# Clearing one column of x^T before it is filled, and forming a combined weight in a stream of its own

## The chip, the cores and the metric

The kernel runs on one core of one Trainium2 chip. The metric is the device time of one execution in microseconds; lower is better. A core has a matrix engine (TensorE, PE in the profile), a vector engine (DVE), a scalar engine (ACT), a general engine (POOL) and a queue processor (SP) that issues DMAs. Each engine works through its own list of instructions in the order in which the program gives them, and an instruction that waits for a semaphore holds up all that stand behind it on its engine.

## What is computed

```python
# q, k, v: (8, 12, 448, 64); w_ch1: (768, 3072); w_ch2: (3072, 768)
scores = q @ k.T / sqrt(64)
x      = (maximum(scores, 0)**2 / 448) @ v          # attention without softmax
x      = x.transpose(0, 2, 1, 3).reshape(8, 448, 768)
u      = x + real(fft(fft(x, axis=1), axis=2))      # Fourier mixing over rows and channels
un     = (u - mean(u)) / sqrt(var(u) + 1e-6)        # over the 768 channels
out    = u + maximum(un @ w_ch1, 0) @ w_ch2
```

## The kernel before

The eight batches go one after the other through attention, mixing, normalization and the feed-forward product (FFN), and the stages of different batches overlap. The FFN works on groups of rows that do not coincide with batches: 384 rows in group 0, 512 in group 1, 384 in group 2 and 256 in each later one.

**Order of the work.** Each activity is a Python generator, here called a stream, that says with `need(engine, duration, deps, bufs)` which engine it wants next, for how long, after which times and with which buffers. A planner (`Streams.run`) picks the piece with the earliest possible start, and among equal starts the one with the lowest rank, and emits its instructions. The planner's clock is its own model; on the chip the engines follow the emitted order, and the semaphores decide when each instruction really starts. So a small edit can change the order of much that comes behind it.

**Attention.** For each batch `b` and each pair of heads `m` (0 to 5), three or fewer score tiles at a time are formed (L734), ACT takes them out of PSUM with a relu (L759, tile `sq`), and DVE or ACT squares them (L774, L771). Eight products with `v` (L716) then give 128 channels of x transposed, in PSUM (`psF`, or `psS` while the FFN's two chains hold both `psF` banks). `leave` in `fold` takes them out, scaled, into `xT` (DVE L553 or ACT L550), in two instructions for the two halves of the sequence. From batch 2 on (`PAR` is 2) each half is written as even and odd positions, 112 of each; the folding that follows reads 113 (`EV`), and column 112 (`EV - 1`) must be zero, since batches 0 and 1 left data there. A DMA transposition then brings each `m` back to row order (SP L650, tile `xn`).

**Folding and mixing.** `halves(b, k)` folds three channel blocks at once: k is 0 for m = 0 to 2 and 1 for m = 3 to 5. It adds and subtracts the halves (DVE L614, L616), then L624 twice, and for k = 1 also L632 and L634, on which the channel transform waits (PE L1210). At batch 2 alone it first clears column 112 of its three blocks (L612). `mix_rows` does the row transform (PE L1024), ACT copies one part (L1036), DVE and POOL form u (L1057, L1059), DVE the statistics (L1066 to L1072), and ACT or POOL the normalized rows (L1085, L1082, tile `un`). These are written to DRAM (`ntop` by SP L1117, `nbot` by POOL L1120) and read back transposed as `unT` (SP L1158); an FFN group starts when its `unT` is there.

**FFN.** The first product (L1445) fills one `psF` bank at a time (there are two), and ACT or DVE takes it out with a relu (L1419, L1417, tile `hT`). Group 0's second product is plain (L1470); groups 1 and 2 form part of theirs by `whole` (L1496), and all other parts are formed by `Pair`, which forms two blocks of rows with seven products of 12 matmuls instead of eight (L1576). Its two chains A and B each keep one `psF` bank; DVE adds what a product gave to the output (L1431), and a chain's next product waits for that add. `Pair` reads sums and differences of blocks of the second weight: `weight_sums` forms them on DVE (L1302, tile `wsum`; the fourth, T[4], lies in the upper half of `hT`). The fourth is formed in twelve blocks after group 1's blocks c = 2 and 3 are done (`upper_free`), and eight of the blocks, which group 2 overwrites, are formed again after its c = 2 (`third_done`). `weight_sums` has rank 6, `halves` 3, the copies ahead of the q and k transpositions (L469, SP L481) 2.

Of the kernel before, what the change touches and what calls it, by code (L numbers as in the profile page):

```python
# [12 lines left out]
ALU = mybir.AluOpType  # L13
# [123 lines left out]
def need(eng, dur, deps=(), bufs=(), ok=None):  # L137
    return eng, dur, list(deps), list(bufs), ok
# [10 lines left out]
def dve(n):  # L149
    return n / 960 + 0.15  # L150
# [6 lines left out]
def dve2(n):  # L157
    return Port(n / 1920 + 0.14)
# [6 lines left out]
def kernel(  # L165
# [9 lines left out]
    nc = tc.nc  # L175
# [7 lines left out]
    JC = FF // 128  # L183
# [9 lines left out]
    PAR, EV = 2, 113  # L193
# [28 lines left out]
    sch = Streams()  # L222
# [68 lines left out]
    half_seq, seq_left, tail_left, half_ready = [None], Cell(), Cell(), Cell()  # L291
# [151 lines left out]
    BX = [Bufs(1) for _ in range(MC)]  # L443
# [79 lines left out]
    def fold(b, m, F, av, give, av_end):  # L523
        one = b < WHOLE
        x, at = xTc[m], av[:, 0:S].rearrange("q (j p) -> q p j", j=4)
        gone = Cell()

        def leave():

            if b < PAR:  # L530
                xa = x[:, 0:HS].rearrange("q (p j) -> q p j", j=4), at[:, 0:R // 2]
                xb = x[:, XH + 1:XH + NS].rearrange("q (p j) -> q p j", j=4), at[:, R - 1:R // 2 - 1:-1, ::-1]
            else:
                split = at.rearrange("q p (h o) -> q o p h", o=2)
                xa = (x[:, 0:256].rearrange("q (o e) -> q o e", o=2)[:, :, 0:R].rearrange("q o (p h) -> q o p h", h=2),
                      split[:, :, 0:R // 2])
                xb = (x[:, XH + 1:XH + 255].rearrange("q (o e) -> q o e", o=2)[:, :, 0:R]
                      .rearrange("q o (p h) -> q o p h", h=2), split[:, :, R - 1:R // 2 - 1:-1, ::-1])
            if b == 0:
                t = yield need("DVE", 2 * dve(HS) + 2 * dve2(NS), [av_end], [BX[m]] + ([BA[m]] if m < 3 else []))  # L540
                for out_, in_ in (xa, xb):
                    nc.vector.tensor_scalar(out_, in_, 1.0 / (64.0 * S), None, op0=ALU.mult)
            else:
                yield need("PE", 0.0, [av_end - LATENCY["PE"]])
                en = "ACT" if sooner(av_end, "ACT", 2 * act(HS), "DVE", 2 * dve(HS)) else "DVE"
                bufs = [BX[m]] + ([BA[m]] if m < 3 and b < PAR else [])
                for out_, in_ in (xa, xb):
                    if en == "ACT":
                        t = yield need(en, act(HS), [av_end], bufs)
                        nc.scalar.activation(out_, in_, AF.Copy, scale=1.0 / (64.0 * S))  # L550
                    else:
                        t = yield need(en, dve(HS), [av_end], bufs)
                        nc.vector.tensor_scalar(out_, in_, 1.0 / (64.0 * S), None, op0=ALU.mult)  # L553
                    bufs = []
                t += LATENCY[en] - LATENCY["DVE"]
            give(t - (0.0 if b else 2 * dve2(NS)))
            if b > 0:
                sch.add(turn_x(b, m, t + LATENCY["DVE"]), (1, 1))
            else:
                x_ready[b][m].t = t + LATENCY["DVE"]  # L560
            gone.t = t
            return t

        if b >= PAR:
            x_gone[b].append(gone)
            sch.add(leave(), (0, 0))
            if m % 3 == 2:
                sch.add(halves(b, m // 3), (3, 3))
            return
        if b == 0:  # L570
            e1 = yield from leave()
        else:
            sch.add(leave(), (0, 0))
            yield need("SP", 0.0, [gone])
            e1 = gone.t + LATENCY["DVE"]
        if one and b:
            e1 = yield need("DVE", 2 * dve2(NS), [e1])
        if m % 3 == 0 and (b == 0 or m == 0):
            trio[:] = [work.tile([128, 3, 2, NS], BF16, name="fold", tag="foldB" if m else "foldA", bufs=1)] + trio[:1]
        f = seq_home[:, SEQ:SEQ + 2 * NS].rearrange("q (t n) -> q t n", t=2) if b and m >= 3 else trio[0][:, m % 3]  # L580
        if not one:
            e1 = yield need("DVE", dve2(NS), [e1])
        nc.vector.tensor_tensor(f[:, 0, :], x[:, 0:NS], x[:, XH:XH + NS], op=ALU.add)
        e1 = yield from next_step(b, "DVE", dve2(NS), e1)
        nc.vector.tensor_tensor(f[:, 1, :], x[:, 0:NS], x[:, XH:XH + NS], op=ALU.subtract)
        F.append(f)
        if b == 0:
            first_folds.append(f)
            f_ready[m].t = e1 + LATENCY["DVE"]
        elif m >= 3:  # L590
            i = m - 3
            e1 = yield need("DVE", (2 if one else 1) * dve2(2 * NS))
            if i == 0:
                trio[:] = [work.tile([128, 3, 2, NS], BF16, name="diff", tag="foldB", bufs=1)]
            t = trio[0][:, i]
            nc.vector.tensor_tensor(t, F[i], f, op=ALU.subtract)
            Bs[b].append(t)
            e1 = yield from next_step(b, "DVE", dve2(2 * NS), e1)
            nc.vector.tensor_tensor(F[i], F[i], f, op=ALU.add)
            As[b].append(F[i])  # L600
            ab_ready[b][i].t = e1 + LATENCY["DVE"]

    x_gone, trio, firsts = [[] for _ in range(B)], [], [None] * B
    BFA, BFB, BFS = Bufs(1), Bufs(1), Bufs(1)

    def halves(b, k):

        x = xT3[k]
        xa, xb = (x[:, :, at:at + 256].rearrange("q m (o e) -> q m o e", o=2)[:, :, :, 0:EV] for at in (0, XH))
        e1 = yield need("DVE", dve2(6 * EV) + 0.1 * (b == PAR), x_gone[b][3 * k:3 * k + 3] + [seq_left], [BFS])  # L610
        if b == PAR:
            nc.vector.memset(x[:, :, EV - 1:EV], 0.0)  # L612
        f = work.tile([128, 3, 2, 2, EV + 1], BF16, name="folds", tag="seqm", bufs=1)
        nc.vector.tensor_tensor(f[:, :, 0, :, 0:EV], xa, xb, op=ALU.add)  # L614
        e1 = yield need("DVE", dve2(6 * EV))
        nc.vector.tensor_tensor(f[:, :, 1, :, 0:EV], xa, xb, op=ALU.subtract)  # L616
        f = f.rearrange("q m t o e -> q (m t) (o e)")
        low = f.rearrange("q c (o e) -> q c o e", o=2)[:, :, :, 0:EH]
        high = f[:, :, 0:2 * EV].rearrange("q c (o e) -> q c o e", o=2)[:, :, :, EV - 1:EH - 2:-1]
        for w, op in enumerate((ALU.add, ALU.subtract)):  # L620
            e1 = yield need("DVE", dve2(12 * EH), [], [(BFA, BFB)[k]] if w == 0 else [])
            if w == 0:
                Y = work.tile([128, 2, 6, 2, EH], BF16, name="fold", tag=("foldA", "foldB")[k], bufs=1)
            nc.vector.tensor_tensor(Y[:, w], low, high, op=op)  # L624
        if k == 0:
            BFS.free.append(e1)
            firsts[b] = Y
            return
        first, second = (y.rearrange("q w c o e -> q (w c o e)") for y in (firsts[b], Y))
        e1 = yield need("DVE", dve2(24 * EH))  # L630
        t = work.tile([128, 24 * EH], BF16, name="diff", tag="seqm", bufs=1)
        nc.vector.tensor_tensor(t, first, second, op=ALU.subtract)  # L632
        e1 = yield need("DVE", dve2(24 * EH))
        nc.vector.tensor_tensor(first, first, second, op=ALU.add)  # L634
        BFB.free.append(e1)
        for y, home in ((first, As), (t, Bs)):
            y = y.rearrange("q (w m t e) -> q w m t e", w=2, m=3, t=2)
            home[b][:] = [y[:, :, m] for m in range(3)]
        for c in ab_ready[b]:
            c.t = e1 + LATENCY["DVE"]  # L640
# [618 lines left out]
    DH = D // 2  # L1259
# [10 lines left out]
    T = [None] * 5  # L1270
    sums = [Cell() for _ in range(5)]
    ffn_begun = [Cell() for _ in range(NGR)]
    unt_left, w2_free, upper_free, third_done = Cell(), Cell(), Cell(), Cell()
# [5 lines left out]
    def weight_sums():  # L1279
# [28 lines left out]
        b11, b12, b21, b22 = (0, 0), (0, 1), (1, 0), (1, 1)  # L1308
# [4 lines left out]
        t2 = yield from home("uA", 4, u_left)  # L1313
# [2 lines left out]
            t2 += yield from home(f"{x}n0", 2, [qk_left])  # L1316
        yield from several(2, t2, t3, b11, ALU.add, [])
        yield from several(1, b12, b12, b11, ALU.subtract, [w2_free])
        yield need("DVE", 0.0, [upper_free])
        t4 = upper(JC * 256, KP, DH)  # L1320
        t4 = [(t4, i) for i in range(KP)]
        yield from several(4, t4, b21, t2, ALU.subtract, [])
        yield need("DVE", 0.0, [third_done])
        T[4], sums[4].t = None, None
        yield from several(4, t4, b21, t2, ALU.subtract, [], JC * 128 // DH)

    def uses():

# [381 lines left out]
```

## Time and profile before

| | us |
|---|---|
| median of 3 runs | 586.08 (585.96 to 586.13) |
| profiled execution, its own time | 588.24 |
| span of the profiled execution | 586.3 |
| PE busy | 571.7 (98%) |
| DVE busy | 412.8 (70%) |
| ACT busy | 330.2 (56%) |
| POOL busy | 137.6 (23%) |

The span runs from the first to the last instruction. The profiled execution is one of its own, 2.16 us over the median. A row of the timeline reads: start, duration, engine, line, operation, output tile and input tile, count, and in brackets the idle time of the engine just before and what ended it. PSUM tiles are `psF` and `psS`.

### The profile page before, as it was taken

Reading aid. Unit: us, or ns where it says so; the run is one execution under the profiler, and the core shown is the slowest. Engines: PE = TensorE matmul, PEld = TensorE weight load, DVE = VectorE, ACT = ScalarE, POOL = GpSimd, SP = SyncE. Lnnn points to the kernel's source line nnn. Section 1 sums busy time; section 2 is a strip of 40 time slices with the busy share of each in tenths; the row PEclk is TensorE's granted clock in tenths of the full one; section 3 lists DMA queues with packets and bytes.
Section 4 is the critical chain, followed back from the end, with each engine's and each line's share of the span. In section 5 each row is a group of like instructions: output and inputs, shape, how many; then the busy total and the mean of one; then the engine's idle time right before and its main releaser. Section 6 shows DMA issues by size and latency. Waiting matters only on the chain.

```text
span 586.3 us, 11457 instructions
## 1 busy us (share of the span) xinstructions
PE 571.7 (98%) x4476; PEld 364.4 (62%) x4476; DVE 412.8 (70%) x929; ACT 330.2 (56%) x503; POOL 137.6 (23%) x190
## 2 busy tenths in 40 slices
PE   8999999999999999999999999999999999999997
PEld 6566556544355446546756667558567686868684
DVE  5978677986679968897899878977946862222222
ACT  5967773687634478777668738766644240404040
POOL 8533121410134211431126132303300230000000
PEclk9999999999999999999999999999999999999999
DMA  9999999875938997599949977995434343131211
GB/s 127 207 210 227 215 226 128 198 108 75 200 48 197 159 179 138 132 193 175 154 103 211 207 139 146 203 164 128 124 75 100 114 144 94 40 91 42 73 36 55
DMA packets 133493, 81.85 MB, mean 140 GB/s; under 512 B 77504, under 2 KB 128704, under 8 KB 133440
## 3 DMA queue, kind: packets, MB, share of 16 engines
q0 software_dynamic: 40320, 33.63, 37.4%
q1 hardware_dynamic: 93120, 47.50, 37.2%
q8 instruction: 35, 0.57, 0.4%
q14 instruction: 18, 0.15, 0.1%
HBM read 62.91 MB, written 26.25 MB: 152 GB/s over the span
## 4 chain that ended last, share of the span: by engine, by line
PE 82%; DVE 8%; ACT 4%; DMA 3%; SPq 1%; issue 1%; POOL 0%; DVEq 0%; POOLq 0%
PE psF L1445 34%; PE psF L1576 24%; PE psS L734 6%; PE psF L716 4%; PE psF L1496 4%; PE psF L1470 3%; PE psS L1210 2%; DVE sq L774 2%; ACT sq L759 2%; DMA xn<-xT 2%; PE psS L716 1%; DMA qkT<-qkr 1%; PE psS L821 1%; PE psS L1024 1%; SPq L1158 1%
## 5 line engine op out<-in xcount | busy, mean ns | idle before, releaser
L1445 PE MATMUL psF<-unT,w 128*128 128x256 bf16 (+2 forms) x1728 | 229.3, 291 | 4.8 <-DVE hT L1417 1.3
L1445 PEld LDWEIGHTS <-w 128*128 128x128 bf16 x1728 | 165.6, 98 | 65.8 <-issue 13.5
L759 ACT ACTIVATE sq<-psS 112x896 bf16<-112x896 f32 x192 | 164.0, 917 | 44.2 <-PE psS L734 44.0
L1419 ACT ACTIVATE hT<-psF 128x512 bf16<-128x512 f32 (+3 forms) x166 | 86.0, 530 | 122.8 <-PE psF L1445 121.4
L774 DVE TENSOR_TENSOR sq<-sq 112x896 bf16<-112x896 bf16 x162 | 102.4, 646 | 16.3 <-ACT sq L759 15.2
L1576 PEld LDWEIGHTS <-hT 128*128 128x128 bf16 x792 | 76.1, 98 | 54.2 <-issue 5.8
L1576 PE MATMUL psF<-w,hT 128*128 128x384 bf16 x462 | 81.5, 326 | 0.3 <-DVE hT L1417 0.2
L1431 DVE TENSOR_TENSOR o<-psF,o 128x384 f32<-128x384 f32 x92 | 50.8, 553 | 42.6 <-PE psF L1576 38.5
L734 PE MATMUL psS<-qkT 64*128 64x448 bf16 (+1 forms) x384 | 51.4, 358 | 1.6 <-ACT sq L759 0.6
L553 DVE TENSOR_SCALAR xT<-psF 128x224 bf16<-128x224 f32 x56 | 19.2, 385 | 28.3 <-PE psF L716 28.2
L1057 POOL TENSOR_TENSOR u<-tp,xn 112x385 f32<-112x385 f32 (+2 forms) x14 | 13.1, 933 | 110.3 <-DVE tp L1039 89.0
L716 PE MATMUL psF<-sq,vn 112*64 112x448 bf16 x312 | 37.0, 358 | 0.0
L376 POOL DMA_DIRECT2D qn<-in_q_dram x21 | 15.7, 748 | 83.1 <-DVE qkr L469 66.1
L1576 PE MATMUL psF<-wsum,hT 128*128 128x384 bf16 x198 | 35.0, 326 | 0.0
L734 PEld LDWEIGHTS <-qkT 64*128 64x128 bf16 (+1 forms) x384 | 15.7, 102 | 28.7 <-issue 21.7
L376 POOL DMA_DIRECT2D vn<-in_v_dram x24 | 17.2, 718 | 65.3 <-PE psS L734 58.6
L716 PEld LDWEIGHTS <-vn 112*64 112x64 bf16 x384 | 17.7, 109 | 21.2 <-issue 13.5
L771 ACT ACTIVATE sq<-sq 112x896 bf16<-112x896 bf16 x30 | 28.6, 957 | 0.5
L1066 DVE BATCH_NORM_STATS2 stats<-u 112x6 f32<-112x384 f32 (+2 forms) x56 | 28.7, 542 | 0.1
L1470 PE MATMUL psF<-w,hT 128*128 128x384 bf16 x144 | 25.1, 326 | 0.0
L1417 DVE TENSOR_SCALAR hT<-psF 128x512 bf16<-128x512 f32 (+3 forms) x38 | 20.4, 550 | 6.3 <-PE psF L1445 5.8
L1085 ACT ACTIVATE un<-u,nmr,rstd 113x768 bf16<-113x768 f32 (+2 forms) x20 | 20.1, 1022 | 8.3 <-DVE nmr L1072 8.2
(166 smaller groups left out, 626.0 us busy)
## 6 DMA issues: line engine op xcount, KB each, us to landing
out_dram<-o SPq DMA_DIRECT2D x56, 192.0 KB
vn<-in_v_dram POOLq DMA_DIRECT2D x24, 224.0 KB, 6.4
qn<-in_q_dram POOLq DMA_DIRECT2D x21, 224.0 KB, 4.6
kn<-in_k_dram POOLq DMA_DIRECT2D x21, 224.0 KB, 6.9
w<-in_moe_w_ch_dram POOLq DMA_DIRECT2D x12, 384.0 KB, 13.2
w<-in_moe_w_ch_dram POOLq DMA_DIRECT2D x4, 1152.0 KB, 27.0
utop<-u SPq DMA_DIRECT2D x12, 336.0 KB
o<-utop SPq DMA_DIRECT2D x16, 192.0 KB
```

The costliest lines, as they stand in the source:

```text
L376: nc.gpsimd.dma_start(out=t, in_=src[b, hs].rearrange("h (p j) d -> p h (j d)", j=4))
L716: nc.tensor.matmul(av[h * Dh:(h + 1) * Dh, 0:S], lhsT=vn[:, c, h0 + h, :], rhs=sq[:, h, :], start=(c == 0), stop=(c == 3))
L734: nc.tensor.matmul(sc[:wide, h, 0:S].rearrange("k (c q) -> k c q", c=4), lhsT=flat[ps, k0:k0 + wide], rhs=qT[ps, m % 2], start=True, stop= ...
L759: nc.scalar.activation(r, sc[:R, :, 0:S], AF.Relu)
L771: nc.scalar.activation(r, r, AF.Square)
L774: nc.vector.tensor_tensor(r, r, r, op=ALU.mult)
L1066: nc.vector.bn_stats(stats[:n, hf, :], u[:n, hf * (D // 2):(hf + 1) * (D // 2)])
L1419: nc.scalar.activation(hs, ps, AF.Relu)
L1431: nc.vector.tensor_tensor(o, pc[:, 0:DH], o, op=ALU.add)
L1445: nc.tensor.matmul(ph[:, i * N:(i + 1) * N], lhsT=w1_sb[m][hf][:, (jj + i) * 128:(jj + i + 1) * 128], rhs=unT[:, m, 0:N], start=(m == 0), ...
L1470: nc.tensor.matmul(pc[:, 0:DH], lhsT=block(j, c), rhs=w2(j, hf), start=(j == 0), stop=(j == JC - 1))
L1576: nc.tensor.matmul(pc[:, 0:DH], lhsT=lhs[i], rhs=rhs[i], start=(start and i == 0), stop=(i == KP - 1), skip_group_check=True)
```

## The change

Three edits:

- At batch 2, `leave` clears column 112 of its own block with a DVE instruction of its own before the two instructions that fill the block, for each m. `halves` no longer clears anything. The buffer `BX[m]`, which the DMA transposition of the batch before gives back, is taken by the clearing instead of by the first filling instruction.
- The fourth combined weight is formed by a stream of its own, `fourth`, of rank 2 instead of 6. `weight_sums` ends once it has added it.
- The two waits in it, for `upper_free` and `third_done`, are put on SP's clock in the planner instead of DVE's. They emit no instruction.

```diff
@@ leave, in fold
                 bufs = [BX[m]] + ([BA[m]] if m < 3 and b < PAR else [])
+                if b == PAR:
+                    yield need("DVE", 0.06, [av_end], [BX[m]])
+                    nc.vector.memset(x[:, EV - 1:EV], 0.0)
+                    bufs = []
                 for out_, in_ in (xa, xb):
@@ halves
-        e1 = yield need("DVE", dve2(6 * EV) + 0.1 * (b == PAR), x_gone[b][3 * k:3 * k + 3] + [seq_left], [BFS])
-        if b == PAR:
-            nc.vector.memset(x[:, :, EV - 1:EV], 0.0)
+        e1 = yield need("DVE", dve2(6 * EV), x_gone[b][3 * k:3 * k + 3] + [seq_left], [BFS])
@@ weight_sums
-        yield need("DVE", 0.0, [upper_free])
+        yield need("SP", 0.0, [upper_free])
         t4 = upper(JC * 256, KP, DH)
         t4 = [(t4, i) for i in range(KP)]
-        yield from several(4, t4, b21, t2, ALU.subtract, [])
-        yield need("DVE", 0.0, [third_done])
-        T[4], sums[4].t = None, None
-        yield from several(4, t4, b21, t2, ALU.subtract, [], JC * 128 // DH)
+
+        def fourth():
+
+            yield from several(4, t4, b21, t2, ALU.subtract, [])
+            yield need("SP", 0.0, [third_done])
+            T[4], sums[4].t = None, None
+            yield from several(4, t4, b21, t2, ALU.subtract, [], JC * 128 // DH)
+
+        sch.add(fourth(), (2, 2))
```

In the order of the built programs, PE's instructions are the same up to the one that starts at 154.18 us in the profile of before, and again from about 322 us to the end. Between the two the same matmuls stand in another order.

## The prediction, made before the changed kernel was run

> **What bounds the kernel now.** I read the page first: the engines' busy time says whether anything but PE can matter.
>
> ```profile
> span 586.3 us, 11457 instructions
> PE 571.7 (98%) x4476; PEld 364.4 (62%) x4476; DVE 412.8 (70%) x929; ACT 330.2 (56%) x503; POOL 137.6 (23%) x190
> ```
>
> PE is idle for 14.6 us in all. The changed program has the same matmuls and the same order of them outside one stretch, so I asked next for the stretch's share (a row gives the stretch, its length, then busy time and count of PE, PEld, DVE, ACT and POOL, the clock and the DMA).
>
> ```profile
> 154.00:322.00 168.00, 164.30 (x1174) 94.91 (x1173) 139.34 (x315) 108.56 (x175) 50.52 (x55) 1.00 0.87 155
> ```
>
> Here PE is idle for 3.70 us at full granted clock. That is the most that the change can bring, 0.6%; what it can cost has no such bound. DVE is busy for 139 of 168 us: a wait on DVE is soon felt.
>
> Then the timeline of the stretch, for PE's gaps. Five make 3.62 us of the 3.70:
>
> ```profile
> 158.54 0.06 DVE L612 MEMSET xT<- 128x3 bf16 x1 [2.68 <-DMA xn<-xT]
> 161.00 0.68 DVE L1417 TENSOR_SCALAR hT<-psF 128x512 bf16<-128x512 f32 x1
> 161.73 4.04 PE L1445 MATMUL psF<-unT,w 128*128 128x512 bf16 x18 [1.26 <-DVE hT L1417]
> 166.13 0.46 PE L1210 MATMUL psS<-chan,fold 128*114 128x193 bf16 x3 [0.36 <-DVE fold L634]
> 204.36 1.14 PE L1445 MATMUL psF<-unT,w 128*128 128x384 bf16 x6 [0.74 <-DVE o L1431]
> 259.23 1.14 PE L1576 MATMUL psF<-w,s 128*128 128x384 bf16 x6 [0.65 <-DVE o L1431]
> 315.19 2.79 PE L1445 MATMUL psF<-unT,w 128*128 128x256 bf16 x24 [0.61 <-DVE mv L1067]
> ```
>
> The first row is what the change touches: the second clearing (m = 3 to 5) writes into blocks that a transposition still reads, so DVE stands still for 2.68 us. The relu at 161.00 waits behind it and holds a `psF` bank, so PE loses 1.26 us, and the folds end late, 0.36 us more. The chain of waits in this stretch says the same:
>
> ```profile
> 152.83 5.55 DMA xn<-xT
> 158.54 0.07 DVE xT L612
> 165.29 0.79 DVE fold L634
> 166.13 2.21 PE psS L1210 x24
> ```
>
> **Part 1: the clearing.** Two instructions of 0.06 us become six, 0.24 us more on DVE, hidden by its idle time. Each stands right before a value block's two exits, and the block that it clears was last read a whole batch earlier, so I expect no wait. The second fold then follows m = 5's exit at once. In the changed order the two relus that DVE takes in group 1's last nine chunks are other ones (the 17th and 21st of 24 instead of the 16th, 17th and 20th), and PE has a value block or scores between. Gain: 1.26 + 0.36 = 1.62 us.
>
> **Part 2: where that time goes.** A PE that doesn't wait only arrives sooner at the next thing. That is group 2's first product, 204.36, which needs `unT`. I walk both sides.
>
> *PE.* Before group 2 the new order holds one value block and two sets of three score tiles more than the old one:
>
> ```profile
> 184.60 0.88 PE psF L716 x8
> 195.53 0.67 PE psS L734 x6
> 192.98 0.48 PE psS L734 x4
> 193.47 2.06 PE psF L1576 x12
> 569.09 13.66 PE psF L1576 x84
> ```
>
> That is 0.88 + 2 x 0.67 = 2.22 us. Taking out the three gaps before (1.26, 0.36, 0.74), PE arrives at 204.36 - 2.36 + 2.22 = 204.2.
>
> *unT.* Its last part comes by this chain:
>
> ```profile
> 187.88 0.16 DVE L1072 SCALAR_TENSOR_TENSOR nmr<-mv,rstd 112x1 f32<-112x1 f32 x1
> 184.97 0.99 POOL L1082 TENSOR_SCALAR un<-u,rstd,nmr 112x768 bf16<-112x768 f32 x1
> 188.13 1.96 POOL L1082 TENSOR_SCALAR un<-u,rstd,nmr 112x768 bf16<-112x768 f32 x1 [2.17 <-DVE nmr L1072]
> 190.37 1.05 POOL L1120 DMA_INDIRECT nbot<-un,backe  x1 [0.28 <-POOL un L1082]
> 195.34 2.51 SPq L1158 DMA_TRANSPOSE unT<-nbot  x1
> 193.29 0.77 POOL L376 DMA_DIRECT2D vn<-in_v_dram  x1 [1.87 <-PE psS L734]
> 195.80 0.94 POOL L376 DMA_DIRECT2D qn<-in_q_dram  x1 [1.74 <-DVE qkr L469]
> ```
>
> L1158 is issued at 195.34 and PE reads at 204.36, 9.02 us later. The gap there is put down to DVE's add, but the transposition may have ended as late as that.
>
> In the new order the second `mix_rows` of batch 2 stands after 60 instead of 42 of the 96 L1496, and the last scale factor behind group 1's last add, two squares and the first pair's sums. Backward from 204.2: 84 products (13.66), two value blocks (1.76), scores (0.48 + 0.67 + 0.48 + 0.67) and four returns to the products (2.06 - 12 x 13.66 / 84 = 0.11 each), 18.2 us, so L1496 ends at 186.0. Then DVE has:
>
> ```profile
> 190.49 0.55 DVE L1431 TENSOR_TENSOR o<-psF,o 128x384 f32<-128x384 f32 x1
> 187.95 0.62 DVE L774 TENSOR_TENSOR sq<-sq 112x896 bf16<-112x896 bf16 x1
> 186.28 0.43 DVE L1560 TENSOR_TENSOR hT<-hT 128x512 bf16<-128x512 bf16 x1
> 187.28 0.29 DVE L1560 TENSOR_TENSOR hT<-hT 128x256 bf16<-128x256 bf16 x1
> 187.69 0.15 DVE L1071 RECIPROCAL rstd<-std 112x1 f32<-112x1 f32 x1
> ```
>
> Two adds, two squares, three sums at 0.43, three at 0.29 and two pairs of 0.15 + 0.16: 5.1 us, so the factor is there at about 191.1 (against 188.04). POOL needs 0.99 to 1.96 us, now issues a q load (0.94) ahead of `nbot`, and pauses 0.28: `nbot` at 193.3 to 194.3. It took 4.97 us from there to L1158 before, so L1158 goes out at 198.3 to 199.3. What a transposition takes when nothing else is in question, the chain shows:
>
> ```profile
> 368.95 5.32 DMA xn<-xT
> 383.78 6.46 DMA qkT<-qkr
> ```
>
> With 5.32 at least and 9.02 at most, `unT` is there between 203.6 and 208.3. PE, ready at 204.2, waits 0 to 4.1 us. I take 1.4: issue at 198.8 and 6.8 us for the transposition, between 6.46 and the old 9.02 and nearer to the first, since the load of v that lay beside it (193.29, after a value block) comes a value block earlier in the new order.
>
> [...]
>
> *The copies.* In the new order the k copy ahead of the q and k transpositions stands before the exit of group 2's first value block, and its L481 behind both L1158 on SP. At another place the trace prices such a wait:
>
> ```profile
> 390.33 0.43 DVE L469 COPY qkr<-kn 112x1024 bf16<-112x1024 bf16 x1 [1.76 <-DMA qkT<-qkr]
> 392.20 1.49 PE L1445 MATMUL psF<-unT,w 128*128 128x256 bf16 x12 [1.02 <-DVE xT L553]
> ```
>
> There PE paid 1.02 us. Here the wait is largely the same time as the wait for `unT`: 0 to 1.02, I take 0.3.
>
> **Part 3: the fourth weight.** Its 20 blocks are the same work on DVE (eleven instructions), earlier in the queue. No product waits for it in the old profile, so nothing is gained by its being early. It now goes ahead of folds, not behind them: the adds that were late before 204.36 and 259.23 stood behind folds and squares, and in the new order the folds stand after them. So 0.74 and 0.65 should go (the first is in PE's arrival above). The moved wait is only in the planner; it can let the first block be queued before the matmuls that it overwrites are done, for 0.5 us at most, while DVE has nothing else.
>
> **Part 4: the rest of the stretch.** The gap of 0.61 comes from a chance:
>
> ```profile
> 311.15 1.80 DVE L1059 TENSOR_TENSOR u<-tp,xn 112x383 f32<-112x383 f32 x1
> 295.76 0.55 DVE L1059 TENSOR_TENSOR u<-tp,xn 113x383 f32<-113x383 f32 x1
> ```
>
> The same instruction takes 1.80 or 0.55 us, by what POOL does beside it. Such things will lie elsewhere: of the 1.26 us after 204.36 (0.65 + 0.61) I expect 0.7 to be lost again, 0 to 2.
>
> **Sum.** -1.62 - 0.74 + 1.4 + 0.3 - 1.26 + 0.7 = -1.22 us. The profiled execution took 588.24 us (the span and 1.94 around it) and becomes 587.02; the median of the runs lies 2.16 lower, 586.08, and becomes 584.86: 584.9. With every term at its lower bound it would be 582.5, with every term at its upper 589.6. A measurement of this kernel tells 0.2% (1.17 us) from no change, so the forecast stands right at that edge.
>
> **The rivals.**
>
> *`unT` in time.* L1158 lands before 204.2. Then -1.62 - 0.74 - 1.26 + 0.7 = -2.92: 583.2. For it: loads of v lie earlier in the new order, so the queues may be emptier. Against: 9.02 before, and no row under 5.32.
>
> *Slower: the way to `unT` decides.* `nbot` now follows a q load in POOL's own DMA queue, and such loads take long to land:
>
> ```profile
> kn<-in_k_dram POOLq DMA_DIRECT2D x21, 224.0 KB, 6.9
> ```
>
> If `nbot`, out at 193.8, needs 6.9 instead of 4.97 us, L1158 goes out at 200.7 and lands, with 9.02, at 209.7; PE waits 5.5 us, less the 2.92: +2.6, 588.7. It beats the gain from a landing at 207.1 on, and is told as slower from 208.3 on. For it: everything on this way is later by 3 us at a point where the old profile had nothing to spare. Against: both prices at their upper ends.
>
> *The wait only changes its name.* The copies of Part 2 hold DVE as at 390.33 and cost 1.02 instead of 0.3: 585.6.
>
> **How the numbers follow.** The forecast gets 0.50, with a range of its own of 583.9 to 585.9; a little over half of it lies below 584.91. `unT` in time 0.20, slower 0.18, the renamed wait 0.12 (a quarter of it slower). Faster 0.27 + 0.20 = 0.47, same 0.23 + 0.09 = 0.32, slower 0.18 + 0.03 = 0.21. For eight in ten I leave out the faster half of the first rival and the upper half of the second: 582.9 to 588.2.
>
> **What would show it.** Right: no clearing with a DMA in brackets, no PE gap between 154 and 200, and PE's first group 2 product preceded by a gap of 0.5 to 3 us, with the last L1158 issued at 198 to 199. `unT` in time: that product without a gap. Slower: L1158 after 200. The copies: an L469 with a DMA in brackets before the first L553 of group 2. Wrong altogether: a new gap of more than 1 us after 215, or a clearing that waits.

## The result, and the profile after

The changed kernel takes 584.3 us (median of 17 runs, 583.1 to 585.8), beside 587.4 us for the kernel before (17 runs, the three ahead of the prediction among them): a ratio of 0.9939, 95% interval 0.9922 to 0.9955. Measured a second time it was 584.1 us, ratio 0.9931 (0.9902 to 0.996). The forecast was 584.9 us and a gain of 0.2%; the time is 0.6 us under it, the gain three times as large.

Much of that difference lies in the kernel before. Its three runs ahead of the prediction lay close together at 586.08 us, while in the later rounds it spread from 585.3 to over 590 us. In 35 runs of the first round of experiments, 19 had a mean granted clock of 0.999 or more (median 586.75) and 16 had less, mostly 0.997 (median 588.96). Of the changed kernel's 29 runs 28 stood at 0.999 or more (medians 584.20 and 584.09). At full clock the medians lie 2.4 us apart (2.6 for the first round of experiments, where the changed kernel did not run beside the old one); the rest of the difference goes with the lower clock of the old kernel's runs. Experiments below show, in profiled executions, pauses of PE of over 2 us with a clock of 0.50 to 0.60 in the 4 us after them; the runs without a trace can't be looked into.

The page of the changed kernel's profiled execution (584.67 us), and the row for the same stretch as in the prediction (stretch, length, busy time and count of PE, PEld, DVE, ACT and POOL, clock, DMA):

```profile
span 582.8 us, 11457 instructions
PE 572.9 (98%) x4476; PEld 365.7 (63%) x4476; DVE 406.4 (70%) x927; ACT 335.0 (57%) x511; POOL 133.7 (23%) x188
...
154.00:322.00 168.00, 167.66 (x1202) 97.89 (x1201) 135.81 (x314) 115.22 (x186) 47.41 (x54) 1.00 0.92 162
```

PE is idle for 0.34 us of the 168, where it was 3.70. The timeline of that stretch has none of the five old gaps, and one small new one:

```profile
156.01 0.06 DVE L549 MEMSET xT<- 128x1 bf16 x1
158.31 0.69 DVE L557 TENSOR_SCALAR xT<-psF 128x224 bf16<-128x224 f32 x2 [2.24 <-PE psF L718]
159.03 0.52 DVE L616 TENSOR_TENSOR folds<-xT 128x678 bf16<-128x678 bf16 x1
161.68 0.69 DVE L1424 TENSOR_SCALAR hT<-psF 128x512 bf16<-128x512 f32 x1
163.54 2.76 PE L1452 MATMUL psF<-unT,w 128*128 128x512 bf16 x12
176.70 0.95 PE L718 MATMUL psF<-sq,vn 112*64 112x448 bf16 x8 [0.27 <-DVE o L1438]
192.60 0.16 DVE L1074 SCALAR_TENSOR_TENSOR nmr<-mv,rstd 112x1 f32<-112x1 f32 x1
194.98 1.17 POOL L1122 DMA_INDIRECT nbot<-un,backe  x1 [0.30 <-issue]
200.13 2.65 SPq L1160 DMA_TRANSPOSE unT<-nbot  x1
206.52 1.14 PE L1452 MATMUL psF<-unT,w 128*128 128x384 bf16 x6
208.20 0.43 DVE L469 COPY qkr<-kn 112x1024 bf16<-112x1024 bf16 x1 [0.29 <-DMA qkT<-qkr]
```

The last of the six clearings (156.01) has no bracket, so DVE does not stand still before it; the fold at 159.03 follows the exit at once; the relu at 161.68 holds nobody up. The first product of group 2 (206.52) has no gap in front of it. All these moments are later by a constant: 1.85 us of the prefix, before anything the change touches, as a value block that both orders share shows (the old kernel, then this one):

```profile
148.63 0.95 PE L716 MATMUL psF<-sq,vn 112*64 112x448 bf16 x8
```

```profile
150.48 0.95 PE L718 MATMUL psF<-sq,vn 112*64 112x448 bf16 x8
```

That delay belongs to this execution, not to the kernel: from 53 to 57 us PE had a clock of 0.61 (1.00 in the old profile), and in a second profile of the changed kernel the same block starts at 149.08.

```profile
53.00:57.00 4.00, 4.00 (x38) 1.97 (x38) 3.14 (x7) 2.10 (x3) 0.00 (x0) 0.61 1.21 225
```

### The profile page after: what moved, and what is told of

It reads as the page before. It is cut to its first block, busy times and chain, and to the rows that moved or that the text cites. A ratio compares the mean times of both kernels' runs of the same rounds, so it can differ in the third digit from the quotient of the medians.

```text
span 582.8 us, 11457 instructions
## 1 busy us (share of the span) xinstructions
PE 572.9 (98%) x4476; PEld 365.7 (63%) x4476; DVE 406.4 (70%) x927; ACT 335.0 (57%) x511; POOL 133.7 (23%) x188
## 4 chain that ended last, share of the span: by engine, by line
PE 88%; DVE 6%; ACT 4%; issue 1%; POOL 0%; DVEq 0%; ACTq 0%; POOLq 0%
PE psF L1452 37%; PE psF L1583 26%; PE psS L736 6%; PE psF L718 5%; PE psF L1503 3%; PE psF L1477 3%; PE psS L1212 2%; ACT sq L761 2%; DVE sq L776 2%; PE psS L718 1%; PE psS L823 1%; PE psS L1026 1%; PE psS L1187 1%; PE psF L505 0%; ACT un L1087 0%
## 5 line engine op out<-in xcount | busy, mean ns | idle before, releaser
L1426 ACT ACTIVATE hT<-psF 128x512 bf16<-128x512 f32 (+3 forms) x169 | 87.9, 532 | 116.6 <-PE psF L1452 115.8
L776 DVE TENSOR_TENSOR sq<-sq 112x896 bf16<-112x896 bf16 x161 | 100.6, 638 | 16.6 <-ACT sq L761 15.6
L1583 PE MATMUL psF<-w,hT 128*128 128x384 bf16 x462 | 81.7, 326 | 0.3 <-DVE hT L1424 0.2
L1087 ACT ACTIVATE un<-u,nmr,rstd 112x768 bf16<-112x768 f32 (+2 forms) x22 | 22.4, 1025 | 7.3 <-DVE nmr L1074 5.0
L1477 PE MATMUL psF<-w,hT 128*128 128x384 bf16 x144 | 25.1, 326 | 0.0
L1503 PE MATMUL psF<-w,hT 128*128 128x384 bf16 x144 | 24.7, 326 | 0.0
```

The source lines that it names most:

```text
L776: nc.vector.tensor_tensor(r, r, r, op=ALU.mult)
L1426: nc.scalar.activation(hs, ps, AF.Relu)
L1477: nc.tensor.matmul(pc[:, 0:DH], lhsT=block(j, c), rhs=w2(j, hf), start=(j == 0), stop=(j == JC - 1))
L1503: nc.tensor.matmul(pc[:, 0:DH], lhsT=block(2 * i + k, c), rhs=weights[i], start=(start and i == 0), stop=(i == KP - 1), skip_group_check=True)
L1583: nc.tensor.matmul(pc[:, 0:DH], lhsT=lhs[i], rhs=rhs[i], start=(start and i == 0), stop=(i == KP - 1), skip_group_check=True)
```

## The experiments

**The two parts alone, and the wait apart from the order.** The changes of order come from the planner, so taking the wait away and reordering the work can be separated. Four kernels, run together.

First, the clearing alone:

```
 # as in the change: memset per m ahead of the exits, with need("DVE", 0.06, ...)
 # not in it: fourth() and its stream
```

> The first part of the change alone: the column is cleared per m ahead of the exits, and the fourth weight stays where it was, in the stream of the first products. The planner makes another order of it, like neither the old nor the new one. Theory 1 (the gain is the DMA wait on DVE that went): the second clearing's 2.68 us are gone, and with them at least the two gaps of PE that they made, 1.26 and 0.36 us; about -1.6 us, ratio 0.9972, whatever the order. Theory 2 (the gain is the new order: what the planner puts ahead of what, the fourth weight included): this order has not the fourth weight early, so gaps of 0.65 and 0.74 us before products whose add stands late on DVE stay or come anew elsewhere, and the time is within 0.5 us of before, or above it. Theory 3 (luck: any order of these streams has its own handful of gaps): a change of either sign, by gaps at places that neither part touches.

Measured: 0.9973 (0.9954 to 0.9992), 586.5 us. The rows of PE with a wait in the stretch, and the copy before the last of them:

```profile
174.86 0.95 PE L718 MATMUL psF<-sq,vn 112*64 112x448 bf16 x8 [0.27 <-DVE o L1433]
203.86 0.48 PE L1578 MATMUL psF<-hT 128*128 128x384 bf16 x2 [0.23 <-DVE hT L1304]
205.20 1.22 PE L1578 MATMUL psF<-hT 128*128 128x384 bf16 x4 [0.85 <-DVE hT L1304]
207.41 0.43 DVE L469 COPY qkr<-kn 112x1024 bf16<-112x1024 bf16 x1 [1.19 <-DMA qkT<-qkr]
208.35 3.08 PE L1447 MATMUL psF<-unT,w 128*128 128x384 bf16 x18 [0.57 <-DVE o L1433]
```

The two gaps of the wait are gone, and the gain is what theory 1 gave for them. But in the order that this part makes by itself, products wait for a combined weight (L1304) that DVE forms late, which happened nowhere in the old profile. In neither profile of the whole change does a product wait for it. So the fourth weight's stream seems to have a use that the prediction didn't see: it keeps a new order from running into the weight.

Second, the fourth weight alone:

```
+        sch.add(fourth(), (2, 2))   # the clearing stays ahead of the folds
```

> The second part alone: the fourth weight by a stream of its own, the clearing by two instructions ahead of the folds as before. The order differs from the old one in some sixty rows of PE only, between the second and third batch's work. Theory 1: the clearing still waits 2.7 us and PE still loses 1.6 us by it; what can go is the 0.74 and the 0.65 us before the two products whose add stood behind folds and squares: 0 to -1.4 us, ratio 0.9976 to 1. Theory 2: the larger part of the whole gain (-2.5 us or more of about -3.6) is here, ratio 0.996. Theory 3: either sign, within 1 us.

The third edit, the two waits put on SP's clock, is in this kernel too; it was not run by itself. Measured: 0.9979 (0.9957 to 1.0001), 587.2 us; whether it gains at all is open. Its profile keeps one gap of 0.61 us at 316 us, and the wait, longer this time. The last row is the stretch after it:

```profile
160.16 0.06 DVE L612 MEMSET xT<- 128x3 bf16 x1 [3.90 <-DMA xn<-xT]
163.35 5.73 PE L1450 MATMUL psF<-unT,w 128*128 128x512 bf16 x18 [2.48 <-DVE hT L1422]
...
163.30:167.30 4.00, 3.95 (x11) 1.45 (x11) 3.97 (x8) 1.40 (x2) 1.46 (x2) 0.60 0.00 0
```

The gaps of 0.74 and 0.65 us are gone, as theory 1 had it, and nothing like theory 2's 2.5 us is gained. For the 0.74 that says little: PE comes to that product so late here that what it needs has long been there (4.4 us, by the table below). The clearing waits 3.90 us for the same transposition for which it waited 2.68 in the old profile, PE pauses for 2.48 us instead of 1.26, and then runs at a clock of 0.60: the same 18 products that took 4.04 us in the old profile take 5.73. The longer wait costs 1.22 and, by the clock, 1.69 us more. It is longer because the transposition went out later, at 154.27 instead of 152.83 (0.4 us of that is delay from before the stretch); it took about as long, 5.73 us against 5.55.

Third, the old order with the wait taken away:

```
+                    if b == PAR and out_ is xa[0]:
+                        nc.vector.memset(x[:, EV - 1:EV], 0.0)   # no need() of its own
-            nc.vector.memset(x[:, :, EV - 1:EV], 0.0)            # halves; its cost of 0.1 stays in the plan
```

> The old kernel's planning in all its costs, so the same order of every instruction on every engine, but the column is cleared per m right ahead of the first exit: on DVE alone two instructions become six and stand earlier; all else is in the old order. Theory 1: the two gaps of 1.26 and 0.36 us go, nothing else changes: -1.6 us, ratio 0.9972. Theory 2: the wait by itself costs little in the end, since PE only arrives sooner at unT and at the adds that are late at 204 and 259 us: 0 to -0.6 us, ratio 0.999 to 1. In the old order unT was wanted at 204.36 at a gap of 0.74 put down to an add; if PE now comes 1.6 us sooner and finds unT missing, that gap grows to 2 us or so and the gain is gone, which is what theory 2 needs.

Measured: 0.9958 (0.994 to 0.9976), 585.4 us. PE's order is the old one, row for row. The product at the old 204.36, the add that the old profile named as ending its gap, and the two gaps that are left:

```profile
201.84 1.14 PE L1444 MATMUL psF<-unT,w 128*128 128x384 bf16 x6
202.10 0.55 DVE L1430 TENSOR_TENSOR o<-psF,o 128x384 f32<-128x384 f32 x1
...
256.71 1.14 PE L1575 MATMUL psF<-w,s 128*128 128x384 bf16 x6 [0.65 <-DVE o L1430]
312.67 2.79 PE L1444 MATMUL psF<-unT,w 128*128 128x256 bf16 x24 [0.62 <-DVE mv L1066]
```

Both gaps of the wait are gone, and so is the 0.74 us, without the fourth weight having moved. What is more, the add now runs after the product has started: the product cannot have been waiting for it. So the 0.74 us were something else, and the next group shows what. Theory 1's price (0.9972) lies inside the interval; theory 2's (0.999 to 1) lies outside.

Fourth, the new order with the wait put back:

```
-                    nc.vector.memset(x[:, EV - 1:EV], 0.0)       # leave; its need() stays in the plan
+            nc.vector.memset(x[:, :, EV - 1:EV], 0.0)            # halves, ahead of the folds
```

> The changed kernel's planning, so its order on PE, ScalarE, GpSimd and SyncE, but the column is cleared by two instructions ahead of the folds as in the old one: the wait for the transposition is back. Theory 1: the clearing for m = 3 to 5 waits 2 to 3 us for a DMA, the relu behind it is late, and PE loses 1 to 1.6 us more than in the changed kernel: ratio to before about 0.9966 (the changed kernel stands at 0.9939). Theory 2: the new order has other work on DVE and PE at that place (two relus of 24 on DVE and a value block or scores between), and takes the wait without a gap: ratio 0.994, as the changed kernel.

Measured: 0.9957 (0.9938 to 0.9976), 585.4 us.

```profile
156.44 0.69 DVE L556 TENSOR_SCALAR xT<-psF 128x224 bf16<-128x224 f32 x2 [2.25 <-PE psF L719]
157.89 0.06 DVE L615 MEMSET xT<- 128x3 bf16 x1 [0.77 <-DMA xn<-xT]
160.35 0.67 DVE L1425 TENSOR_SCALAR hT<-psF 128x512 bf16<-128x512 f32 x1
...
318.49 1.47 PE L1453 MATMUL psF<-unT,w 128*128 128x256 bf16 x12 [0.22 <-DVE xT L556]
320.56 1.47 PE L1453 MATMUL psF<-unT,w 128*128 128x256 bf16 x12 [0.60 <-DVE hT L1425]
```

In the new order the exit of m = 5 comes later (156.44 instead of 155.17), so the transposition is nearly done when the clearing gets there: 0.77 us of wait instead of 2.68, and no gap of PE. In this execution the new order alone hides the wait, against theory 1. The time does not decide: its interval holds both forecasts, and this execution (583.55 us) is one of the fastest of its 12 (median 585.4), so whether the order also hides a longer wait is not shown. The third kernel shows the other way: the wait alone can be removed in the old order. Each of the two is worth 0.42 to 0.43%, and the changed kernel's 0.61% is less than their sum, as it should be if both remove the same loss. Whether it is more than either is not settled by these intervals, which overlap.

**Who meets whom at group 2's first product.** Three kernels and the changed one again, run together. One GpSimd instruction, the normalised rows `un` that `nbot` is stored from, is written several times over, which delays the last part of `unT` and leaves the order of all instructions as it is:

```
-                nc.gpsimd.tensor_scalar(un[:n], u[:n], ...)
+                for _ in range(3 if b == 2 and ch == 1 and i == 1 else 1):
+                    nc.gpsimd.tensor_scalar(un[:n], u[:n], ...)
```

> The changed kernel as it is, again, on the chip and in the rounds of the three others, as the measure for them. Expected 0.994 of before (0.9939 so far). Its profile tells which readings of the first one hold: that PE's first product of group 2 starts within 0.3 us of the landing of unT (theory U: unT and PE arrive together), that no clearing waits, and whether the gap near 391 us, outside the changed stretch, is there (1.02 us in the old profile, none in the changed one; theory 3 has it come and go with no link to the change).

Measured: 0.9931, 584.1 us. No clearing waits in its profile, and the gap at 391 us is not there. That gap comes and goes: the old order has it in the old profile (1.02 us) and in the third kernel (0.45), but not in the old kernel with `unT` later, below; the new order lacks it in both profiles of the changed kernel and has it with the rows `un` written three times (0.57). So it is no part of the change. But the changed kernel's profiled execution, the slowest of its 12 (585.86 us), does what the forecast said and the first profile did not:

```profile
193.58 1.18 POOL L1122 DMA_INDIRECT nbot<-un,backe  x1 [0.30 <-issue]
200.49 2.43 SPq L1160 DMA_TRANSPOSE unT<-nbot  x1
206.23 1.14 PE L1452 MATMUL psF<-unT,w 128*128 128x384 bf16 x6 [1.18 <-DVE sq L776]
319.41 0.43 DVE L469 COPY qkr<-kn 112x1024 bf16<-112x1024 bf16 x1 [3.67 <-DMA qkT<-qkr]
320.49 1.47 PE L1452 MATMUL psF<-unT,w 128*128 128x256 bf16 x12 [0.46 <-DVE xT L557]
322.56 1.47 PE L1452 MATMUL psF<-unT,w 128*128 128x256 bf16 x12 [0.60 <-DVE hT L1424]
```

PE waits 1.18 us before group 2's first product, and 1.06 us are lost again at 320 us, behind a k copy that holds DVE for 3.67. The profile names DVE's squares for the 1.18. The semaphore events of the traces give another account (last of the sixteen increments of the last transposition of `unT`, us from the start):

```
kernel                 issued   landed    product starts   behind the landing
before                 195.34   204.227   204.362          0.135
changed                200.13   206.388   206.523          0.135
changed, second time   200.49   206.091   206.23           0.14
old order, no wait     193.89   201.708   201.843          0.135
new order, wait back   198.38   204.020   204.413          0.39
fourth weight alone    197.05   201.845   206.20           4.4
```

In four of the six the product starts 0.135 to 0.14 us after the landing, as it does in all four kernels below that delay `unT`. In the old kernel too: the 0.74 us that ended at 204.36, put down to the add (203.78 to 204.33), were a wait for `unT`.

> The changed kernel, with one instruction on GpSimd done three times over (the same normalised rows un of batch 2's second half, written again to the same place): the store of nbot and the last transposition of unT go out later by 2 x 1.09 = 2.2 us, nothing else is moved. Theory U (unT lands 0.1 us before PE takes it, so PE's arrival and unT's landing are both at the bound): PE stands 2 to 2.5 us before group 2's first product, and the time is up by about 2.2 us against the changed kernel (ratio to before about 0.9977). Rival (the product follows its predecessor, and the landing beside it is chance with slack behind it): less than 0.5 us.

Measured: 587.1 us, 3.0 more than the changed kernel in the same rounds (0.9983, interval 0.9951 to 1.0015); its seven runs at full clock have a median of 585.4, 1.3 more.

```profile
206.86 1.74 PE L1453 MATMUL psF<-unT,w 128*128 128x384 bf16 x6 [2.22 <-DMA unT<-nbot]
...
206.80:210.80 4.00, 3.94 (x18) 1.30 (x18) 0.95 (x3) 0.59 (x3) 1.00 (x2) 0.57 1.10 219
```

The gap is there, 2.22 us, and the profile now names the transposition. Theory U holds; and again a clock of 0.57 after it, which makes the six products cost 1.74 instead of 1.14.

> The old kernel with the same instruction done three times over, so unT later by 2 x 0.99 to 2 x 1.96 = 2.0 to 3.9 us. The old profile has 0.74 us of idle PE before group 2's first product and names VectorE's add as what ended it. Theory U (it was unT, which landed at 204.23, 0.13 us before the product): the gap grows one for one, to 2.7 to 4.6 us, and the time by 2 to 4 us, ratio 1.0034 to 1.0068. Rival, as my prediction had it (the add ended it, unT had been there for a while): the first part of the delay is free, the gap grows by less than 1 us.

Measured: 589.6 us, ratio 1.0025 (0.9991 to 1.006). The clearing, which is unchanged here, waited longer than in the old profile:

```profile
159.91 0.06 DVE L612 MEMSET xT<- 128x3 bf16 x1 [3.80 <-DMA xn<-xT]
163.10 5.73 PE L1446 MATMUL psF<-unT,w 128*128 128x512 bf16 x18 [2.38 <-DVE hT L1418]
...
206.27 0.55 DVE L1432 TENSOR_TENSOR o<-psF,o 128x384 f32<-128x384 f32 x1
207.37 1.14 PE L1446 MATMUL psF<-unT,w 128*128 128x384 bf16 x6 [1.26 <-DMA unT<-nbot]
```

The gap is 1.26 us, not the 2.7 to 4.6 expected: PE itself came 2.5 us later (the gap opens at 206.11 instead of 203.62), after a pause of 2.38 us behind that clearing and 18 products that took 5.73 us instead of 4.04. The gap grew by 0.52 us, which is the rival's number and not theory U's. But what ends it is `unT`, which landed 0.135 us before the product, while the add was over at 206.82, half a microsecond before. So theory U missed the size and has the cause; the rival has the size by the accident of the longer pause.

> The order of the kernel with the fourth weight alone (some sixty rows of PE from the old order), and the column cleared per m right ahead of the first exit, without a place of its own in the planning: both parts in their effect, without the large reordering that the clearing's own steps brought. Of the old profile's gaps the two of the wait (1.26, 0.36), the 0.74 and the 0.65 should be gone. Theory 1 (the two effects are the gain, the new order is a bystander): as the changed kernel, 0.994 to 0.995. Theory 2 (the large reordering has a share of its own): at least 0.002 above the changed kernel, 0.996 or more.

Its edits are the third kernel's and the fourth weight's stream. Measured: 0.9941 (0.9909 to 0.9973), 583.9 us, as the changed kernel.

```profile
164.79 0.46 PE L1209 MATMUL psS<-chan,fold 128*114 128x193 bf16 x3 [0.19 <-DVE fold L633]
...
202.13 1.14 PE L1449 MATMUL psF<-unT,w 128*128 128x384 bf16 x6
...
312.15 2.79 PE L1449 MATMUL psF<-unT,w 128*128 128x256 bf16 x24 [0.62 <-DVE mv L1066]
```

The 0.65 us at 257 us, still there in the third kernel, are gone, as they were with the fourth weight alone; of the 0.36, 0.19 are left. The time is theory 1's: the clearing's own steps in the plan, which cause the large reordering, add nothing that these intervals could show.

**What a pause costs.** The same instruction twice and six times, to tell a short pause from a long one.

> The changed kernel with the rows un of batch 2's second half written twice instead of once (three times was 2.2 us of idle PE before group 2's first product, and TensorE's granted clock at 0.57 in the 4 us after it). Theory C (a short pause of PE costs itself alone, and one of over 2 us costs 1.6 us more, since the clock is granted at half for the next 3.4 us): the pause is 1.1 us longer than the changed kernel's own 0.1 to 1.2, so 1.2 to 2.3 us, mostly under the point where the clock goes: +1.1 us on the changed kernel at full clock, 585.2, and few runs at a mean clock of 0.997. Rival (the clock has nothing to do with the pause's length): the share of runs at 0.997 is as in the changed kernel or as in the old one, whatever the pause.

Measured: 586.7 us, 0.9963 (0.9939 to 0.9987); the six of 12 runs at 0.999 or more have a median of 584.95.

```profile
206.21 1.14 PE L1453 MATMUL psF<-unT,w 128*128 128x384 bf16 x6 [1.46 <-DVE qkr L469]
...
206.20:210.20 4.00, 3.99 (x28) 1.96 (x29) 1.73 (x6) 2.19 (x4) 1.40 (x2) 1.00 1.05 213
```

> The changed kernel with the same rows written six times: unT later by 5 x 1.1 to 5 x 1.3 = 5.5 to 6.5 us. Theory C: the pause before group 2's first product is 5 to 7 us in every run, so the clock goes in every run: 584.1 + 5.5 to 6.5 + 1.6 = 591 to 592 us, mean clock 0.997 in all or nearly all runs, granted clock near 0.57 in the 4 us after the pause. Rival: full clock in most runs, and 589.6 to 590.6 us.

Measured: 592.9 us, 1.0071 (1.0047 to 1.0096); none of its 9 runs has a mean clock over 0.997.

```profile
210.37 2.08 PE L1453 MATMUL psF<-unT,w 128*128 128x384 bf16 x6 [4.86 <-DMA unT<-nbot]
...
208.40:210.30 1.90, 0.00 (x0) 0.00 (x0) 0.00 (x0) 0.00 (x0) 0.00 (x0) 0.50 1.01 228
210.30:214.30 4.00, 3.93 (x16) 1.42 (x18) 0.00 (x0) 0.55 (x2) 0.00 (x0) 0.50 1.54 204
```

After a pause of 1.46 us the clock stays at 1.00, after 4.86 it is 0.50. That a long pause is followed by a lower clock held in all four profiles that show one of over 2 us (2.22, 2.38, 2.48 and 4.86 us, then 0.50 to 0.60). The sizes did not hold. With the longer delay the clock falls while PE still stands (it is 0.50 from 208.4 us on) and stays so until 215.1 us, twice the 3.4 us that theory C had. The pause was a little short of its 5 to 7 us and the time still above its 591 to 592 us, and six of the nine runs had a mean clock of 0.994 and two 0.991, not 0.997. With the shorter delay six of 12 runs lost clock, not few. That share is also what the rival allowed, as in the old kernel; what speaks against the rival is the longer delay, where every run lost clock. Since the pause of one execution differs from the next (none printed in the changed kernel's first profile, 1.18 us in its second), the six may have had pauses over 2 us; the runs without a trace don't show it.

## Why the prediction was right, and where it was not

**The ceiling was too low.** I took PE's gaps as the profile prints them. A group of the changed kernel's rows says that one product of 384 columns lasts 326 ns:

```profile
L1452 PE MATMUL psF<-unT,w x24: 323/326/337, 206.5 to 211.9; 128*128 128x384 bf16 x24
```

In the prediction's row 84 such products take 13.66 us, one every 163 ns. Each record reaches 163 ns into the next one, so a gap behind such a product is printed 0.16 us shorter than the time lost. For five gaps that is an estimated 0.8 us of gain that the sum left out.

**Part 1 (−1.62)** was right: both gaps go as soon as the wait goes, in the old order and in the new (0.19 us of the second is left in one of the kernels). It was a price for one execution, though. The wait was 2.68 us in the old profile and 3.80 and 3.90 in two others that have the same clearing at the same place, and there PE lost 2.38 and 2.48 us and then clock (0.57 and 0.60 in the 4 us after). That can explain why the old kernel's runs spread, and why the gain over all runs is larger than the gain at full clock. It is not shown for the runs without a trace, and it is not the only way to lose clock: four of 12 runs of the clearing alone lost it too, without that wait.

**Part 2, the way to `unT`,** was walked correctly and one term was mis-sized. With the 1.85 us of delay taken off, the scale factor was there at 190.9 (predicted 191.1), `nbot` went out at 193.1 (193.3 to 194.3), L1160 at 198.3 (198.3 to 199.3), and PE was ready at 204.6 (204.2). The transposition took 6.25 us, not 6.8, so the wait of 1.4 became 0.1: the rival "`unT` in time", by a tenth of a microsecond. In the second profile the store of `nbot` took 6.91 us from issue to L1160 (193.58 to 200.49) instead of 4.97, and the wait was 1.18. So one profiled execution did what the first rival said and the other what the forecast said; how often each happens in the other runs is not shown. The slower rival had one of its two prices right in that second execution, the 6.9 us, and its sign, L1158 after 200; but the transposition then took 5.6, not 9.02.

For this transposition the profiles show 4.5 us (the rows `un` written six times) to 8.9 us (the old kernel), so the 5.32 us that the prediction took as its least was too high.

**The old 0.74 us** was misread. The prediction saw that the old transposition might have landed as late as PE's read, and then believed the profile's releaser, the add, and gave the gain to Part 3. In the old order without the wait the gap went with the fourth weight in its place. It belongs to `unT`, and is the same term as Part 2. The sum does not suffer by it: when PE is ready without the gap is the same, whatever ended it.

**The copies (0.3)**: DVE waited 0.29 us at 208.20 and PE did not notice. A later copy of the same kind cost PE more where I had not looked: at 320 us in the second profile (3.67 us of wait on DVE, 1.06 on PE).

**Part 3**: the 0.65 us goes whenever the fourth weight has its own stream, as predicted (in the order of the clearing alone it is not there either). That no product waits for the fourth weight did not hold in the order of the clearing alone. **Part 4**: 0.7 us lost again were 0.27 in the first profile and 1.33 (0.27 + 0.46 + 0.60) in the second.

**The sum.** From printed gaps the first profile gives −3.62 + 0.35 = −3.3 us for the stretch, the second −3.62 + 2.51 = −1.1, against −1.22 forecast. The length itself can be read off too, since all orders share the value block at 148.63 and one behind the stretch (the old kernel, the changed one, the changed one again):

```profile
325.22 0.95 PE L716 MATMUL psF<-sq,vn 112*64 112x448 bf16 x8
```

```profile
323.00 0.95 PE L718 MATMUL psF<-sq,vn 112*64 112x448 bf16 x8
```

```profile
323.96 0.95 PE L718 MATMUL psF<-sq,vn 112*64 112x448 bf16 x8
```

From block to block it is 176.59 us in the old profile, 172.52 in the first of the changed kernel and 174.88 in the second: −4.07 and −1.71. Behind it both are about 1.2 us shorter, by the gap at 391 us, which has nothing to do with the change.

So the nearness of the forecast (584.9 against 584.3) is in part luck. From profiled execution to profiled execution the time fell by 3.57 us (588.24 to 584.67), not by 1.22; and the step from there down to the median was 0.37 us, not the 2.16 that the old kernel's three runs gave. The two errors largely cancel. Behind the second is one of level: three runs at 586.08 stood for a kernel whose median over 17 runs was 587.4, with about half of its executions in the later rounds at a lower clock.

## What to carry to other kernels

When a profile names an engine whose instruction ended just before a product, look at when the product's transfer landed, and ask for an order in which the two come apart: here the same 0.74 us changed owner. Price a wait on a transfer by more than one execution: the transposition of `unT` took 4.5 to 8.9 us from profile to profile, and the clearing that waits for another one started at 159.91 and 160.16 us in two profiles, at 158.54 in a third. In the four profiles here with a PE pause of over 2 us the products behind it were slow as well (18 of them took 5.73 us after 2.38 and 2.48 us, 4.04 after 1.26; six took 1.74 after 2.22 and 2.08 after 4.86, 1.14 after 1.18), and 28 of the changed kernel's 29 runs kept full clock, where about half of the old kernel's did.

## What was not expected of the hardware

Pauses of PE of 1.18, 1.26 and 1.46 us were followed by a granted clock of 1.00, pauses of 2.22, 2.38, 2.48 and 4.86 us by 0.50 to 0.60 in the 4 us after them. After the three shorter of these the clock falls 0.4 to 0.7 us after PE resumes (the first products after the 2.48 us are still 215 ns apart, the following ones 427) and is back 3.4 us later; that cost 1.7 us after the 2.48. In the pause of 4.86 us it falls about 2 us before PE resumes and is back 6.8 us later, twice as long.

So the clock stayed at 1.00 after 1.46 us and fell after 2.22 us; no profile here shows a pause between the two, and none shows what sets the 3.4 and 6.8 us or whether the same pause always costs the same clock. The 0.61 from 53 to 57 us in the changed kernel's first profile followed no pause of over 1 us (the longest before it, 0.98 us, ended at 51.49, and the clock fell at 53.90), though it too lasted 3.4 us; why is left open.
